# First expert's count and closing moved behind the mask multiplications, its tokens turned behind those of step 32

## The chip, the cores and the metric

One core of one Trainium2 chip runs the kernel. The metric is the device time of one execution in microseconds (us), as the median of several runs; less is better. The engines are named as in the profile: PE (TensorE matmul), PEld (its weight load), DVE (VectorE), ACT (ScalarE), POOL (GpSimd), SP (SyncE). DVE, ACT and POOL take their instructions in the order of the program.

## What is computed

Retention attention (8 batches, 8 heads, 576 positions, head size 64: scores with a decaying causal mask), whose output is read as 4608 tokens of 512 numbers, and then a mixture of 16 experts in 4 groups of 4. Each token goes to one expert: the best group, then the best expert in it.

```python
scores = scale * np.matmul(q, k.transpose(0, 1, 3, 2))
ret = scores * Dmat[None, :, :, :]          # gamma ** (i - j) for i >= j, else 0
x = np.matmul(ret, v)                       # turned to 4608 x 512
...
g_idx = np.argmax(x @ w_group, axis=1)
e_idx = np.argmax(xg @ w_expert[g], axis=1)
...
h = np.maximum(xg[mask_e] @ w1[g, e], 0.0)
ye = h @ w2[g, e]
out[tok_idx] = combined[:, None] * ye       # product of the two softmax weights
```

All in float32. An expert's layers are 512 by 1024 and 1024 by 512.

## The kernel before

The tokens are cut into 36 tiles of 128. A first loop over t (line 859) makes the attention, software-pipelined over the steps: in step t the scores of tile t + 1 are made by PE in the one PSUM tile `pss` (`scores`), and DVE multiplies them with the causal mask into `sT` (`masked`, two instructions). PE makes the products of tile t - 1 in the one PSUM tile pair `px` (`av` and `inter`), and DVE scales and copies them into `xT` (`turned`). `state` carries the sum over keys and values in `pst`, which ACT copies. Three tiles make a group: some steps behind its last tile, `logits` and `gate_pe` (PE), `choose` and `weigh` (DVE, with an exponential on ACT), and `places_pe` and `places` give each token of the group its expert and its row. POOL then stores the tokens, ordered by expert, in `xs` in HBM (`xnat_store`, an indirect DMA).

The experts' work begins before the last tiles are done. With PICK = 23, step 28 (r = 5) picks the expert with the most tokens so far (`pick(0)`), and its first 256 tokens (EARLY) are worked on as pass 0. Step 29 (r = 6) counts them and fixes them: `taken` is six small DVE instructions and one indirect DMA on POOL, which writes zeros over the rows behind the expert's last token (`xpad(0)`); `close` is three DVE instructions, which raise that expert's count so that later tokens stay apart from the early ones. Step 30 (r = 7) loads the expert's tokens from `xs` into `xb` (`xload(0)`, four DMAs on SP's queue and a small one for the tokens' numbers), and from there on each step loads a piece of weights (`load_piece`, two DMAs on SP's queue). Step 31 makes a mask of ids (`without`). Steps 34 and 35 (r = 11 and 12) turn `xb` into `xTf` by two block transposes on DVE (`xturn(0, 0, 2)` and `xturn(0, 1, 2)`). Step 34 also picks the second expert (`pick(1)`). The last step of the attention but one makes the first piece of the first layer (`layer1(0, 0)`, PE, line 598), which reads `xTf`.

Each engine but PE keeps the order in which the code is written (`pin`, line 94, which is also the line L117 that the profile shows for all of DVE, ACT, POOL and SP); PE's is fixed as well (`manual_schedule`). Waits between engines follow from the tiles that an instruction reads and writes. Behind the first loop come 16 passes over the experts and a last one for the rest of the first expert's tokens, in which nearly all time goes into matmuls.

Of the kernel before, what the change touches and what calls it, by code (L numbers as in the profile page):

```python
# [65 lines left out]
def moe_retention(ctx, tc, qk, kv, wgt, w1, w2, c_f, out):  # L66
# [117 lines left out]
    def ring(name):  # L184

        return gp.tile([P, NB * WQ], F32, name=name, tag="ring", bufs=4)

    def nblocks(p):
        return -(-CS[p] // 32)
# [4 lines left out]
    def xpair(nm):  # L194
        return [
            gp.tile([P, NKC, CMAX], F32R, name=f"xT{x_}_{nm}", tag="xT" + x_, bufs=2) for x_ in "hl"
        ]
# [63 lines left out]
    def xpad(p):  # L261

        row = apart("xs", pool.indirect_dma_start(
            out=xs, out_offset=bass.IndirectOffsetOnAxis(ap={0: pad0, 1: pad1}.get(p, pads[:, p % E : p % E + 1]), axis=0),
            in_=zero, in_offset=None, bounds_check=E * NS - 1, oob_is_err=False,
        ))
        if p == 1:
            placed.append(row)

    def pad(rows, e, n, cap):  # L270

        pd = sm.tile([P, 2], F32, name=f"pd_{rows.name}", tag="pd")
        dve.tensor_scalar(pd[:, 0:1], sln[:, 0:1], n, None, ALU.add)
        dve.tensor_scalar(pd[:, 1:2], pd[:, 0:1], float(cap), float(E * NS), ALU.is_ge, ALU.mult)
        dve.tensor_tensor(pd[:, 0:1], pd[:, 0:1], pd[:, 1:2], ALU.add)
        dve.scalar_tensor_tensor(rows, e, float(NS), pd[:, 0:1], ALU.mult, ALU.add)
# [4 lines left out]
    def xturn(p, part, of):  # L281

        if part == 0:
            xTs[p] = xpair(f"m{p}")
            if p == 0:

                xTf[p] = wp.tile([P, NKC, EARLY], F32, name="xTf_0", tag="wl1", bufs=3)
            else:
                xTf[p] = ring(f"xTf_{p}")[:, 0 : NKC * CMAX].rearrange("p (k c) -> p k c", k=NKC)
        nb = nblocks(p)  # L290
        b0, b1 = nb * part // of, nb * (part + 1) // of
        dve.transpose(
            xTf[p][:, :, 32 * b0 : 32 * b1].rearrange("p k (b t) -> p b k t", t=32),
            xg[p][:, b0:b1, 0:DQ].rearrange("p b (k f) -> p b k f", f=32),
        )
# [179 lines left out]
    def counted():  # L475

        return obs[-1][:, 0, :]
# [76 lines left out]
    def taken():  # L554

        f0, pc = picked[0]
        k2 = sm.tile([P, E], F32, name="k2")
        dve.tensor_tensor(k2, eah[0], pc, ALU.mult)
        c0 = sm.tile([P, 1], F32, name="c0")
        dve.tensor_reduce(c0, k2, AX.X, ALU.add)  # L560
        pad(pad0, f0, c0, EARLY)
        xpad(0)
        picked["c0"] = c0

    def close():

        c0 = picked["c0"]
        c2 = sm.tile([P, 1], F32, name="c2")
        dve.tensor_tensor(c2, room, c0, ALU.subtract)
        dve.tensor_scalar(c2, c2, 0.0, 2.0, ALU.max, ALU.min)  # L570
        dve.scalar_tensor_tensor(counted(), eah[0], c2, counted(), ALU.mult, ALU.add)
# [65 lines left out]
    with ExitStack() as ac:  # L637
# [41 lines left out]
        def more_masks():  # L679

            dve.tensor_copy(masks[:, 1], masks[:, 0])
            for par in range(2):
                dve.memset(masks[par * D : par * D + D, 1, par, D:P], 0.0)
# [11 lines left out]
        def make_gq(c):  # L695
            w = P if c < 4 else D
            for j in range(0, P, w):
                dve.tensor_tensor(
                    gqs[c][:, :, j : j + w], gqs[0][:, :, 0:w],
                    gc[:, c].unsqueeze(2).to_broadcast([P, 4, w]), ALU.mult,  # L700
                )
# [23 lines left out]
        def late_consts(t):  # L725
            if 0 < t < 5:
                make_gq(t)
            if t == 5:
                more_masks()
            if t == 3:  # L730
                dve.tensor_copy(ensb, cf[:, KC_ENS : KC_ENS + E])
                more_counts()
                dve.memset(counted(), 0.0)
                dve.memset(zero, 0.0)
# [39 lines left out]
        def masked(t):  # L774
            T = tiles[t]
            T["sT"] = ap.tile([P, 2, NP, P], F32, name=f"sT_{t}", tag="sT")
            mask = masks[:, T["m"]].unsqueeze(1).to_broadcast([P, 2, 2, P])
            for o in range(2):
                dve.tensor_tensor(
                    T["sT"][:, o].rearrange("p (i a) j -> p i a j", a=2),  # L780
                    pss[:, o].rearrange("p (i a j) -> p i a j", i=2, a=2), mask, ALU.mult,
                )
# [76 lines left out]
        for t in range(NT + 1):  # L859
            if t + LOADS - 1 < NT:  # L860
                loads(t + LOADS - 1, "a")
            now = t < NT
            r = t - PICK

            if last_of_group(t - 4):
                choose(t - 4)
            if last_of_group(t - 5):
                places(t - 5)
            if r == 8:
                without()  # L870
            if r in (11, 12):
                xturn(0, r - 11, 2)
            if t + 1 < NT:
                scale(t + 1)
            if t:
                av(t - 1)
            if t + LOADS - 1 < NT:
                loads(t + LOADS - 1, "b")
            if now:
                state(t)  # L880
            if t:
                inter(t - 1)
                turned(t - 1)
            if r == 6:
                taken()
                close()
            if last_of_group(t - 4):
                weigh(t - 4)
            if t + 1 < NT:
                scores(t + 1)  # L890
                masked(t + 1)
            late_consts(t)
            if now and 6 <= t:
                xnat_pe(t - 6)
                xnat_out(t - 6)
            if now and last_of_group(t - 2):
                logits(t - 2)
            if last_of_group(t - 3):
                gate_pe(t - 3)
            if now and last_of_group(t - 4):  # L900
                places_pe(t - 4)

            u = t - 6
            while 0 <= u and "sl" in tiles[tiles[u]["grp"][-1]] and not tiles[u].get("out"):
                tiles[u]["out"] = True
                u -= 1
            for u in range(max(u + 1, 0), t - 5):
                if now:
                    xnat_store(u)
            if r == 5:  # L910
                pick(0)
                expert_of(0)


            if r == 7:
                xload(0)
            if r == 11:
                pick(1)
                expert_of(1)
            if r > 6:  # L920
                load_piece(r - 7)
            if t == NT - 1:

                layer1(0, 0)
            if t == NT:
                ids(0)
# [576 lines left out]
```

## Time and profile before

| | us |
|---|---|
| median of 3 runs | 587.57 |
| lowest, highest | 586.05, 915.11 |
| profiled execution | 589.62 |
| its span, first to last instruction | 587.8 |
| PE busy in it | 571.2 (97%) |
| DVE busy in it | 425.8 (72%) |
| steps 28 to 35 in it | about 117 to 148 |

The timeline gives, for one engine, its instructions in order of time; like instructions that follow each other are one row with a count, and the length is from the first's start to the last's end. An instruction may start a little before the one ahead of it on its engine has ended. A wait that the profile puts down as "issue" is one for nothing that the profile shows. SPq is the queue that issues transfers; the length of such a row is that of issuing, not of the transfer.

### The profile page before, as it was taken

How to read it: one execution, taken by the hardware profiler on the slowest of the kernel's cores; microseconds unless marked ns; L12 is line 12 of the kernel's file. 1: busy time of each engine (PE TensorE's matmuls, PEld its weight loads, DVE VectorE, ACT ScalarE, POOL GpSimd, SP SyncE). 2: the span in 40 equal slices, each digit the busy share in tenths (PEclk: the TensorE clock that was granted, in tenths of full speed). 3: DMA queues.
4: the chain of work that ended last, by engine and by line, in shares of the span. 5: the costliest groups of instructions: out<-in, count | busy, mean ns of one | idle time of the engine just before them, and what ended most of it. 6: DMA issues, size and time to landing. Idle time of an engine off the chain costs nothing.

```text
span 587.8 us, 16858 instructions
## 1 busy us (share of the span) xinstructions
PE 571.2 (97%) x6057; PEld 535.8 (91%) x6057; DVE 425.8 (72%) x1003; ACT 326.3 (56%) x853; POOL 259.7 (44%) x391
## 2 busy tenths in 40 slices
PE   7999999999999999999999999999999999999994
PEld 5878788877779999999999999999999999999992
DVE  4877677788688768876768586776868768676782
ACT  5677777776456544454545454554545545455462
POOL 0022333233413046555564837355474654835643
PEclk7999999999999999999999999999999999999998
DMA  8999998979874944746656483937557494683921
GB/s 327 405 378 328 323 366 328 331 243 372 309 234 147 282 186 115 277 121 266 188 200 202 192 285 125 326 103 285 164 223 259 147 327 141 254 302 89 385 92 36
DMA packets 62410, 141.98 MB, mean 242 GB/s; under 512 B 9425, under 2 KB 30297, under 8 KB 62304
## 3 DMA queue, kind: packets, MB, share of 16 engines
q1 hardware_dynamic: 52944, 120.19, 59.0%
q0 software_dynamic: 9216, 20.28, 9.5%
q8 instruction: 73, 1.20, 0.8%
q14 instruction: 33, 0.27, 0.1%
q10 hardware_dynamic: 144, 0.05, 0.0%
HBM read 120.22 MB, written 24.81 MB: 247 GB/s over the span
## 4 chain that ended last, share of the span: by engine, by line
PE 87%; DVE 5%; issue 3%; DMA 2%; ACT 1%; POOL 1%; SPq 0%; POOLq 0%; DVEq 0%; another core or an unknown queue 0%
PE ph L612 31%; PE py L1016 10%; PE py L1018 10%; PE py L1017 10%; PE px L812 6%; PE pss L768 4%; PE pxt L378 3%; PE px L830 3%; PE pst L797 2%; PE pss L756 2%; PE plt L422 1%; DVE wl L117 1%; DVE sT L117 1%; POOL out L117 1%; PE ph L598 1%
## 5 line engine op out<-in xcount | busy, mean ns | idle before, releaser
L117 POOL DMA_INDIRECT out<-y,ii x151 | 164.0, 1086 | 66.4 <-issue 31.5
L117 DVE TENSOR_TENSOR wl<-r,wh 128x512 fp32r<-128x512 f32 x264 | 169.9, 685 | 5.8 <-ACT xt_last L117 2.6
L117 ACT ACTIVATE hh<-ph 128x256 fp32r<-128x256 f32 (+15 forms) x128 | 53.7, 420 | 200.4 <-PE ph L612 128.9
L117 ACT CAST wh<-r 128x512 fp32r<-128x512 f32 x264 | 149.1, 617 | 0.0
L612 PE MATMUL ph<-xTl_m,wh 128*128 128x324 f32 (+16 forms) x496 | 146.8, 296 | 0.3 <-DVE xTl_m L117 0.2
L612 PE MATMUL ph<-xTh_m,wh 128*128 128x324 f32 (+16 forms) x496 | 147.1, 297 | 0.0
L612 PE MATMUL ph<-xTh_m,wl 128*128 128x324 f32 (+16 forms) x496 | 146.6, 296 | 0.0
L1016 PE MATMUL py<-hh,wh 128*128 128x320 f32 (+19 forms) x480 | 143.0, 298 | 0.6 <-ACT hh L117 0.4
L1018 PE MATMUL py<-hl,wh 128*128 128x332 f32 (+14 forms) x480 | 142.2, 296 | 0.4 <-DVE hl L117 0.4
L1017 PE MATMUL py<-hh,wl 128*128 128x332 f32 (+14 forms) x480 | 141.8, 295 | 0.0
L117 DVE SCALAR_TENSOR_TENSOR hl<-ph,hh 128x256 fp32r<-128x256 f32 (+14 forms) x124 | 57.8, 467 | 99.9 <-ACT hh L117 54.9
L612 PEld LDWEIGHTS ph<-xTl_m,wh 128*128 128x128 f32 x496 | 93.6, 189 | 1.2 <-DVE xTl_m L117 0.7
L612 PEld LDWEIGHTS ph<-xTh_m,wh 128*128 128x128 f32 x496 | 93.6, 189 | 0.4 <-issue 0.2
L612 PEld LDWEIGHTS ph<-xTh_m,wl 128*128 128x128 f32 x496 | 93.7, 189 | 0.0
L117 POOL COPY pace<-hh 1x1 f32<-1x1 f32 x140 | 34.4, 246 | 131.8 <-ACT hh L117 120.9
L1016 PEld LDWEIGHTS py<-hh,wh 128*128 128x128 f32 x480 | 90.6, 189 | 1.3 <-ACT hh L117 1.2
L1018 PEld LDWEIGHTS py<-hl,wh 128*128 128x128 f32 x480 | 90.4, 188 | 0.9 <-DVE hl L117 0.9
L1017 PEld LDWEIGHTS py<-hh,wl 128*128 128x128 f32 x480 | 90.7, 189 | 0.0
L117 POOL DMA_INDIRECT xs<-xt,sl x33 | 32.7, 991 | 104.7 <-DVE xT L117 43.3
L117 ACT ACTIVATE vs<-b,cf 128x64 f32<-128x64 f32 x288 | 72.4, 336 | 8.0 <-DMA b<-in_kv 6.7
L117 DVE TENSOR_TENSOR sT<-pss,masks 128x512 f32<-128x512 f32 x72 | 46.0, 680 | 12.8 <-PE pss L756 7.0
L812 PE MATMUL px<-sT,vs 128*64 128x128 f32 x576 | 40.3, 283 | 0.1
(194 smaller groups left out, 614.3 us busy)
## 6 DMA issues: line engine op xcount, KB each, us to landing
r<-in_w SPq DMA_DIRECT2D x138, 512.0 KB
a<-in_qk SPq DMA_DIRECT2D x35, 512.0 KB
b<-in_kv SPq DMA_DIRECT2D x31, 512.0 KB
xb<-xs SPq DMA_DIRECT2D x20, 165.0 KB
xb<-xs SPq DMA_DIRECT2D x20, 148.5 KB
out<-y,ii POOLq DMA_INDIRECT x151
xb<-xs SPq DMA_DIRECT2D x12, 181.5 KB
b<-in_kv SPq DMA_DIRECT2D x6, 256.0 KB
```

The source lines that it names most:

```text
L117: i_ = f(*a, **k)
L378: pe.transpose(T["pxt"][:, i, :], T["xT"][:, i, :], ident)
L422: pe.matmul(plt[32 * i : 32 * i + 32], wgp[:, i, :], tiles[t]["xTg"][:, i], start=True, stop=True)
L612: pe.matmul(ph[:, :w], a[:, kc, cs], b[:, kc, :w], start=n == 0, stop=n == 3 * NKC - 1)
L756: pe.matmul(pss[:, o, i * P : i * P + P], T["kT"][r, i, :], T["qT"][r, i, :], start=True, stop=True,)
L768: pe.matmul(pss[k_, o, (i + par) * P + late * D : (i + par) * P + to], T["kT"][r, i + par, k_], T["qT"][r, i + par, late * D : to], start= ...
L797: pe.matmul(pst[o * D : o * D + D, i, :], T["k"][:, h, :], T["vs"][:, h, :], start=first and i == 0, stop=True, skip_group_check=True,)
L812: pe.matmul(px[g * D : g * D + D, o, s * P : s * P + P], T["vs"][:, 4 * s + 2 * g + o, :], T["sT"][:, o, 2 * s + g, :], start=s == 0, stop ...
L830: pe.matmul(px[g * D : g * D + D, o, s * P + r * w : s * P + r * w + w], st[rows, 2 * s + g, :], T["qT"][rows, 2 * s + g, r * w : r * w + ...
L1016: pe.matmul(py[:, :w0], wh[:, f % 2, ds_], hh[:, :w0], start=st_, stop=False)
L1017: pe.matmul(py[:, :w], wl[:, f % 2, ds_], hh[:, :w], start=False, stop=False)
L1018: pe.matmul(py[:, :w], wh[:, f % 2, ds_], hl[:, :w], start=False, stop=sp_)
```

## The change

In step 29, `taken` and `close` are written behind `scores` and `masked` of that step, which were ahead of `weigh` and `scores`. In step 32 (r = 9), behind its `scores` and `masked`, both transposes of the first expert's tokens follow each other; in steps 34 and 35 they are gone. Nothing is added or left out.

```diff
--- before.py
+++ after.py
@@ -868,8 +868,6 @@
                 places(t - 5)
             if r == 8:
                 without()
-            if r in (11, 12):
-                xturn(0, r - 11, 2)
             if t + 1 < NT:
                 scale(t + 1)
             if t:
@@ -881,14 +879,17 @@
             if t:
                 inter(t - 1)
                 turned(t - 1)
-            if r == 6:
-                taken()
-                close()
             if last_of_group(t - 4):
                 weigh(t - 4)
             if t + 1 < NT:
                 scores(t + 1)
                 masked(t + 1)
+            if r == 6:
+                taken()
+                close()
+            if r == 9:
+                xturn(0, 0, 2)
+                xturn(0, 1, 2)
             late_consts(t)
             if now and 6 <= t:
                 xnat_pe(t - 6)
```

PE, ACT, POOL and SP keep their order. On DVE two places change. The first is step 29, before the change. xT_27 from px_28 is the turn of tile 28, k2 to ob_8 are `taken` and `close`, sT_30 the two masks of tile 30, lg_26 the first instruction of `choose` for the group of tiles 24 to 26:

```order
L117 TENSOR_TENSOR xT_27_2417<-px_28_2492,gq1_115 128x4x128
L117 TENSOR_TENSOR k2_2522<-e0h_68,pc0_2459 128x16
L117 TENSOR_REDUCE c0_2524<-k2_2522 128x1
L117 TENSOR_SCALAR pd_pad0_79_2526<-cf_64,c0_2524 128x1
L117 TENSOR_SCALAR pd_pad0_79_2526<-pd_pad0_79_2526 128x1
L117 TENSOR_TENSOR pd_pad0_79_2526<-pd_pad0_79_2526 128x1
L117 SCALAR_TENSOR_TENSOR pad0_79<-f00_2468,pd_pad0_79_2526 128x1
L117 TENSOR_TENSOR c2_2534<-cf_64,c0_2524 128x1
L117 TENSOR_SCALAR c2_2534<-c2_2534 128x1
L117 SCALAR_TENSOR_TENSOR ob_8_2385<-e0h_68,c2_2534,ob_8_2385 128x16
L117 TENSOR_TENSOR sT_30_2554<-pss_109,masks_113 128x512 x2
L117 TENSOR_REDUCE lg_26_2572<-pl_26_2565 128x60
```

And with the change:

```order
L117 TENSOR_TENSOR xT_27_2417<-px_28_2492,gq1_115 128x4x128
L117 TENSOR_TENSOR sT_30_2538<-pss_109,masks_113 128x512 x2
L117 TENSOR_TENSOR k2_2541<-e0h_68,pc0_2459 128x16
L117 TENSOR_REDUCE c0_2543<-k2_2541 128x1
L117 TENSOR_SCALAR pd_pad0_79_2545<-cf_64,c0_2543 128x1
L117 TENSOR_SCALAR pd_pad0_79_2545<-pd_pad0_79_2545 128x1
L117 TENSOR_TENSOR pd_pad0_79_2545<-pd_pad0_79_2545 128x1
L117 SCALAR_TENSOR_TENSOR pad0_79<-f00_2468,pd_pad0_79_2545 128x1
L117 TENSOR_TENSOR c2_2553<-cf_64,c0_2543 128x1
L117 TENSOR_SCALAR c2_2553<-c2_2553 128x1
L117 SCALAR_TENSOR_TENSOR ob_8_2385<-e0h_68,c2_2553,ob_8_2385 128x16
L117 TENSOR_REDUCE lg_26_2572<-pl_26_2565 128x60
```

The masks of tile 30 moved ahead of the nine instructions; what stands behind both is the same. The second place is the end of step 32 and the start of step 33, before the change. lg_29 to ob_9 are `choose` for the group of tiles 27 to 29, xT_30 from px_32 is the turn of tile 32:

```order
L117 TENSOR_TENSOR sT_33_2811<-pss_109,masks_113 128x512 x2
L117 TENSOR_REDUCE lg_29_2834<-pl_29_2823 128x60
L117 TENSOR_REDUCE mx_29_2836<-lg_29_2834 128x15
L117 TENSOR_TENSOR df_29_2838<-lg_29_2834,mx_29_2836 128x60
L117 SCALAR_TENSOR_TENSOR oh_29_2842<-df_29_2838,cf_64 128x60
L117 TENSOR_REDUCE m2_29_2844<-oh_29_2842 128x15
L117 TENSOR_TENSOR oh_29_2842<-oh_29_2842,m2_29_2844 128x60
L117 TENSOR_TENSOR ob_9_2680<-oh_29_2842 128x48
L117 TENSOR_TENSOR xT_30_2720<-px_32_2857,gq1_115 128x4x128
```

With the change:

```order
L117 TENSOR_TENSOR sT_33_2811<-pss_109,masks_113 128x512 x2
L117 STREAM_TRANSPOSE xTf_0_2816<-xb_0_2665 128x4x4x32 x2
L117 TENSOR_REDUCE lg_29_2839<-pl_29_2828 128x60
L117 TENSOR_REDUCE mx_29_2841<-lg_29_2839 128x15
L117 TENSOR_TENSOR df_29_2843<-lg_29_2839,mx_29_2841 128x60
L117 SCALAR_TENSOR_TENSOR oh_29_2847<-df_29_2843,cf_64 128x60
L117 TENSOR_REDUCE m2_29_2849<-oh_29_2847 128x15
L117 TENSOR_TENSOR oh_29_2847<-oh_29_2847,m2_29_2849 128x60
L117 TENSOR_TENSOR ob_9_2680<-oh_29_2847 128x48
```

The two transposes (xTf_0) came in between the masks of tile 33 and `choose`. In steps 34 and 35 they stood, before the change, like this (k01 to e1i are `pick(1)`):

```order
L117 TENSOR_REDUCE ob_10_2935<-ob_9_2680 128x16
L117 STREAM_TRANSPOSE xTf_0_2939<-xb_0_2665 128x4x4x32
L117 TENSOR_TENSOR xT_33_2977<-px_33_2950,gq2_116 128x4x128
L117 TENSOR_TENSOR sT_35_2995<-pss_109,masks_113 128x512 x2
L117 SCALAR_TENSOR_TENSOR k01_3021<-pc1_3019,cf_64 128x16
L117 SCALAR_TENSOR_TENSOR k01_3021<-e0h_68,k01_3021 128x16
L117 TENSOR_REDUCE m01_3024<-k01_3021 128x1
L117 TENSOR_SCALAR e1h_69<-k01_3021,m01_3024 128x16
L117 TENSOR_TENSOR k11_3027<-e1h_69,cf_64 128x16
L117 TENSOR_REDUCE f01_3029<-k11_3027 128x1
L117 CAST e1i_71<-f01_3029 128x1
L117 STREAM_TRANSPOSE xTf_0_2939<-xb_0_2665 128x4x4x32
```

With the change both are gone there, and the rest follows in the same order:

```order
L117 TENSOR_REDUCE ob_10_2940<-ob_9_2680 128x16
L117 TENSOR_TENSOR xT_33_2978<-px_33_2951,gq2_116 128x4x128
L117 TENSOR_TENSOR sT_35_2996<-pss_109,masks_113 128x512 x2
L117 SCALAR_TENSOR_TENSOR k01_3022<-pc1_3020,cf_64 128x16
L117 SCALAR_TENSOR_TENSOR k01_3022<-e0h_68,k01_3022 128x16
L117 TENSOR_REDUCE m01_3025<-k01_3022 128x1
L117 TENSOR_SCALAR e1h_69<-k01_3022,m01_3025 128x16
L117 TENSOR_TENSOR k11_3028<-e1h_69,cf_64 128x16
L117 TENSOR_REDUCE f01_3030<-k11_3028 128x1
L117 CAST e1i_71<-f01_3030 128x1
L117 TENSOR_TENSOR xT_33_2978<-px_34_3047,gq3_117 128x4x128
```

## Rows read from the trace of the kernel before

**Rows 1.** The page of the profile: the span, PE's and PEld's busy time, PE's busy share in 40 equal slices in tenths, the queue that brings instructions (packets, MB, share of 16 engines), and the engines' shares of the chain that ended last.

```profile
span 587.8 us, 16858 instructions
...
PE 571.2 (97%) x6057; PEld 535.8 (91%) x6057; DVE 425.8 (72%) x1003; ACT 326.3 (56%) x853; POOL 259.7 (44%) x391
...
PE   7999999999999999999999999999999999999994
...
q8 instruction: 73, 1.20, 0.8%
...
PE 87%; DVE 5%; issue 3%; DMA 2%; ACT 1%; POOL 1%; SPq 0%; POOLq 0%; DVEq 0%; another core or an unknown queue 0%
```

**Rows 2.** Timeline of DVE from 121 to 130 us, steps 29 to 31. Columns: start and length in us, engine, line and operation, out<-in with its shape, count, and in brackets the engine's idle time before it and what ended that. The row at 121.64 is the first instruction of `taken`, the one at 123.13 the last of `close`.

```profile
121.03 0.69 DVE L117 TENSOR_TENSOR xT<-px,gq 128x512 f32<-128x512 f32 x1 [1.07 <-PE px L830]
121.64 0.16 DVE L117 TENSOR_TENSOR k<-e0h,pc 128x16 f32<-128x16 f32 x1
...
123.13 0.23 DVE L117 SCALAR_TENSOR_TENSOR ob<-e0h,c,ob 128x16 bf16<-128x16 f32 x1
123.28 1.28 DVE L117 TENSOR_TENSOR sT<-pss,masks 128x512 f32<-128x512 f32 x2
124.48 0.40 DVE L117 TENSOR_REDUCE lg<-pl 128x60 f32<-128x240 f32 x1
...
127.84 1.26 DVE L117 TENSOR_TENSOR sT<-pss,masks 128x512 f32<-128x512 f32 x2
```

**Rows 3.** Timeline of PE from 120 to 130 us, columns as above; L768 are the scores, L830 the products with the state.

```profile
120.56 1.02 PE L768 MATMUL pss<-a 64*64 64x128 f32 x32
...
123.91 0.67 PE L830 MATMUL px<-a,st 64*64 64x128 f32 x16
124.61 0.91 PE L768 MATMUL pss<-a 64*64 64x128 f32 x13
125.94 0.68 PE L768 MATMUL pss<-a 64*64 64x64 f32 x19 [0.42 <-issue]
...
128.75 0.67 PE L830 MATMUL px<-a,st 64*64 64x128 f32 x16
129.24 0.85 PE L768 MATMUL pss<-a 64*64 64x128 f32 x32
```

**Rows 4.** Waits between 123.5 and 126 us: who waited for whom, us in total, times, the longest.

```profile
PEld pss L768 <- DVE sT L117: 0.3, 1, 0.3
```

**Rows 5.** Timeline of POOL: the pad of the first expert and the store behind it.

```profile
123.11 0.97 POOL L117 DMA_INDIRECT xs<-zero,pad  x1 [2.69 <-DVE c L117]
...
124.55 0.99 POOL L117 DMA_INDIRECT xs<-xt,sl  x1 [0.28 <-POOL xt L117]
```

**Rows 6.** Timeline of SP's queue from 123 to 176 us: start and length of the issuing, and the count. xb at 127.62 is the first expert's tokens, xb at 166.26 the next expert's; r are weights.

```profile
127.62 2.14 SPq L117 DMA_DIRECT2D xb<-xs  x4
...
130.81 20.06 SPq L117 DMA_DIRECT2D r<-in_w  x14
166.26 1.89 SPq L117 DMA_DIRECT2D xb<-xs  x4
```

**Rows 7.** Waits of SP's queue between 123 and 140 us, columns as in rows 4.

```profile
SPq L117 <- DMA xs<-xt,sl: 4.1, 1, 4.1
SPq L117 <- PE px L830: 3.3, 1, 3.3
```

**Rows 8.** Timeline of DVE from 134 to 173 us, columns as in rows 2. The first two rows of xTf are the transposes that the change moves, the last is the next expert's.

```profile
134.27 1.29 DVE L117 TENSOR_TENSOR sT<-pss,masks 128x512 f32<-128x512 f32 x2 [1.05 <-PE pss L768]
135.47 0.40 DVE L117 TENSOR_REDUCE lg<-pl 128x60 f32<-128x240 f32 x1
...
137.22 0.21 DVE L117 TENSOR_TENSOR ob<-oh 128x48 bf16<-128x48 f32 x1
137.92 0.69 DVE L117 TENSOR_TENSOR xT<-px,gq 128x512 f32<-128x512 f32 x1 [0.49 <-PE px L830]
...
139.46 1.26 DVE L117 TENSOR_TENSOR sT<-pss,masks 128x512 f32<-128x512 f32 x2
...
141.40 0.71 DVE L117 STREAM_TRANSPOSE xTf<-xb 128x512 f32<-128x512 f32 x1 [0.16 <-issue]
...
145.17 0.70 DVE L117 STREAM_TRANSPOSE xTf<-xb 128x512 f32<-128x512 f32 x1
...
172.58 1.30 DVE L117 STREAM_TRANSPOSE xTf<-xb 128x512 f32<-128x512 f32 x2 [1.01 <-DMA xb<-xs]
```

**Rows 9.** Timeline of PE from 139 to 148 us; L812 are the products of the masked scores with the values, L797 the state, L435 turns the gate's logits, L598 is `layer1(0, 0)`.

```profile
139.02 1.09 PE L812 MATMUL px<-sT,vs 128*64 128x128 f32 x16
139.94 0.63 PE L797 MATMUL pst<-vs,b 128*64 128x64 f32 x16
...
140.99 0.64 PE L768 MATMUL pss<-a 64*64 64x64 f32 x32
...
145.17 0.49 PE L435 MATMUL pl<-cf,lt 128*128 128x128 f32 x3
145.93 1.99 PE L598 MATMUL ph<-xTf,r 128*128 128x256 f32 x8 [0.27 <-DVE xTf L117]
```

**Rows 10.** Timeline of ACT from 136 to 139 us: the exponential inside `choose`, and the copy of the state.

```profile
136.41 0.25 ACT L117 ACTIVATE ex<-df 128x60 f32<-128x60 f32 x1 [0.77 <-DVE df L117]
...
138.48 0.34 ACT L117 COPY st<-pst 128x256 f32<-128x256 f32 x1
```

## The prediction

> **What bounds the kernel now.** I read the page first. PE is busy for 97% of a span of 587.8 us, and 87% of the chain that ended last is PE; DVE has 5% of it [rows 1]. So a change on DVE is worth what PE stops waiting for, and nothing else. I therefore looked at the places where PE waits for DVE in the steps that are edited, about 120 to 147 us into the span. There are two.
>
> The first is in step 29. DVE turns px of tile 28 at 121.03, then does the nine small instructions of `taken` and `close` (from 121.64 to 123.36), and only then masks the scores of tile 30 (123.28 to 124.56) [rows 2]. PE has a single `pss`: it wrote those scores from 120.56 to 121.58 and can't write tile 31's before DVE has read them. Tile 31's scores begin at 124.61, 0.05 us after the mask ends [rows 3], and the weight load ahead of them waited 0.3 us for sT [rows 4]. The reader is to see that the nine instructions are long, and that the wait they make on PE is short: PE had other work until 124.4.
>
> The second is before `layer1(0, 0)`: its first matmul at 145.93 waited 0.27 us for the second transpose of the first expert's tokens, which DVE did from 145.17 to 145.87 [rows 8, 9].
>
> **Part 1: the count and closing go behind the mask.** DVE does the same nine instructions and two mask multiplications in another order, so it reaches the first instruction of `choose` at 124.48 either way. The mask of tile 30 starts when its scores are there, behind the turn, at 121.64, which is 1.64 us earlier. What PE gets of that: elsewhere its scores start 0.49 us after the product with the state ahead of them (128.75 to 129.24); in step 29 it was 0.70 us (123.91 to 124.61) [rows 3]. So PE wins 0.21 us. It doesn't keep it: one step later DVE, which has not moved, masks tile 31 from 127.84 to 129.10 [rows 2], and with the same 0.05 us of handing over PE can't start tile 32's scores before 129.15. Before they started at 129.24. What is left is **-0.09 us**. Ends of this term: 0 and the 0.3 us of the wait [rows 4]; the nine instructions whole, 1.64 us, would be the most that could be had if PE had nothing else to do.
>
> PE's own gaps in that place bear on it too: in tile 31's scores there is a gap of 0.42 us with "issue" as its cause, between 125.52 and 125.94 [rows 3], in which it waits for nothing that the profile shows. If that gap stays where it is in time, even the 0.21 us is lost there, and the term is 0. [...]
>
> **What part 1 makes late.** `taken` issues a DMA, the pad of the first expert. Nine instructions start later by the mask, 1.20 us (123.28 to 124.48). POOL issues the pad at 123.11 and the store of tile 23's tokens behind it at 124.55 [rows 5]; both move by 1.20. On SP the load of the first expert's tokens (`xload(0)`) waited 4.1 us for such a store's landing [rows 7] and went out at 127.62 [rows 6]; it moves to 128.82, and with it the weight loads queued behind it, from 130.81. Two of the first expert's eight weight loads wait for PE anyway (3.3 us [rows 7]), so the queue is level again there. The first weights are wanted at 145.93, 15 us after the first load's issue. So this costs 0; if the cover were gone it would cost PE up to 1.20 us.
>
> **Part 2: both transposes go ahead of `choose` of step 33.** They leave the places at 141.40 (0.71 us) and 145.17 (0.70 us) and stand behind the mask of tile 33 [rows 8]. Side by side two take 1.30 us (the row at 172.58), and a DVE instruction starts about 0.08 us before the one ahead of it ends (124.48 against 124.56), so what follows moves by 1.22 us. In a row:
> - `choose` starts at 136.69 instead of 135.47, and its last instruction ends at 138.65 instead of 137.43.
> - The turn of tile 32 was idle 0.49 us for PE before its start at 137.92. That idle time takes part of the shift: it starts at 138.57, 0.65 us late, and ends at 139.26.
> - PE has one px. Its products of tile 33 at 139.02 [rows 9] must wait for that turn: about 139.31, 0.29 us late.
> - The mask of tile 34 starts at 139.46 + 0.65 = 140.11 and ends at 141.37. PE's scores of tile 35, at 140.99 before [rows 9], start at 141.42: **+0.43 us** (this holds the 0.29).
> - ACT's exponential of that `choose` moves from 136.41 to 137.63, and the copy of the state behind the eight scalings from 138.48 to 139.70, ending at 140.05 [rows 10]. PE's next state product stood at 139.94 and now stands at 140.23, so it isn't held, with 0.18 us to spare.
> - From there DVE is ahead: it has no transpose in its next two steps. `layer1(0, 0)` finds its tokens done since about 136.8, so its wait goes: **-0.27 us**.
>
> Without the overlap of 0.08 us (shift 1.30, the turn 0.81 late) the scores come at 141.58, +0.59; with all of it hidden behind other work of PE it is 0. I take 0.43 since it goes by starts, as the rows show them.
>
> Whether the tokens are there in time: no row shows when they landed, since the transposes were too late to wait. The next expert's load bounds it from above: issued from 166.26 to 168.15, its tokens, 12 blocks of 32 against 8, let the transpose begin at 172.58 [rows 6, 8]. That is 6.32 us from the first issue, 4.43 from the end of the last. With 128.82, and 127.62 + 2.14 + 1.20 = 130.96, the first expert's land by 135.14 to 135.39; the transposes come up at about 135.39. So no wait, by a margin near zero on that bound and of several us if landing is quick. [...]
>
> **The sum**: -0.09 + 0.43 - 0.27 = +0.07 us. The profiled execution took 589.62 us around its span of 587.8; with the change 589.7. The median of the runs is 587.57, 2.05 us less; the same sum there gives 587.6. From the second of the 40 slices to the last but one PE is busy for nine tenths or more [rows 1], so what is won or lost there reaches the end nearly whole.
>
> **Rivals.**
> - *Faster*: the shift of `choose` is hidden. Then the wait before `layer1(0, 0)` goes for nothing (-0.27) and the wait of step 29 whole (-0.3): 587.0. For it: both waits are on record [rows 4, 9]. Against it: there is one `pss` and one px, and the mask of tile 34 would have to end by about 140.94; it ended at 140.72 before, so only 0.2 us of a shift are free.
> - *Slower*: DVE takes its instructions in order, and if the tokens land after 135.4 the transposes hold `choose`, the turn of tile 32 and the masks. Its price is one us per us of lateness. If the landing is later by the whole 1.20 us that part 1 adds, the sum is +1.3: 588.8. For it: the bound of the next expert's load leaves no margin. Against it: that load is half as large again, and was issued beside other traffic.
> - *It doesn't do what it says*: the 0.42 us gap takes part 1's lead, and both masks of tiles 34 and 35 hold PE as before: the terms cancel within 0.2 us, 587.8. This can't be told from the forecast by the time, only in the trace.
>
> **How the numbers follow.** Forecast with the third rival: 0.64. Faster by half a us or more: 0.18. Slower by that: 0.14. Something that these rows don't show, of more than 2%: 0.04. Two per cent are 11.8 us, about what a measurement of this kernel can tell from no change, and over forty times the wait before `layer1(0, 0)`; so the chances are faster 0.02, within 2% 0.96, slower 0.02. The range goes from the nine instructions won whole, 587.57 - 1.64 = 585.9, to the transposes lost whole, 587.57 + 1.22 = 588.8; it also takes in the spread of the two low runs, 586.05 and 587.57. The forecast's own range is 587.0 to 588.0.
>
> **What would show it.** In the changed trace: tile 31's scores without a wait for sT, starting at about 124.4; tile 32's still at about 129.15; the pad about 1.2 us later, and the token load with it; two transposes side by side ahead of `choose` without a wait for DMA; the turn of tile 32 without a wait for PE, and PE waiting for DVE at tile 35's scores; no wait for xTf at `layer1(0, 0)`, which starts within 0.3 us of 145.93. Wrong would be: a DMA wait at the transposes, or `layer1(0, 0)` more than 0.5 us off.

## The result, and the profile after

Median after 591.44 us (588.48 to 595.64, 20 runs), before on the same chip 587.96: ratio 1.0054, 95% interval 1.0034 to 1.0073. The kernel became about half a per cent slower, 3.2 us by that ratio (the two medians lie 3.5 us apart), which is within 2% but outside the range of the prediction: 587.57 by that ratio is 590.7, where 588.8 was the upper end.

The page of the changed kernel, profiled in an execution of 590.35 us; its lines answer to [rows 1]:

```profile
span 588.6 us, 16856 instructions
...
PE 570.3 (97%) x6057; PEld 534.3 (91%) x6057; DVE 426.7 (72%) x1003; ACT 326.8 (56%) x853; POOL 257.9 (44%) x391
...
PE   7999999998999999999999999999999999999995
...
PE 85%; DMA 5%; DVE 3%; issue 3%; ACT 2%; POOL 1%; SPq 1%; POOLq 0%; DVEq 0%; ACTq 0%
```

PE does the same work, but one slice (the tenth, around 140 us) has fallen from 9 to 8, and DMA has 5% of the chain of work where it had 2%. The timeline of DVE shows both edits; the rows at 121.39 to 124.08 answer to [rows 2], the others to [rows 8]:

```profile
120.72 0.69 DVE L117 TENSOR_TENSOR xT<-px,gq 128x512 f32<-128x512 f32 x1 [1.06 <-PE px L830]
121.39 1.29 DVE L117 TENSOR_TENSOR sT<-pss,masks 128x512 f32<-128x512 f32 x2
122.60 0.16 DVE L117 TENSOR_TENSOR k<-e0h,pc 128x16 f32<-128x16 f32 x1
...
124.08 0.23 DVE L117 SCALAR_TENSOR_TENSOR ob<-e0h,c,ob 128x16 bf16<-128x16 f32 x1
...
133.83 1.29 DVE L117 TENSOR_TENSOR sT<-pss,masks 128x512 f32<-128x512 f32 x2 [0.89 <-PE pss L768]
137.27 1.30 DVE L117 STREAM_TRANSPOSE xTf<-xb 128x512 f32<-128x512 f32 x2 [2.15 <-issue]
138.50 0.37 DVE L117 TENSOR_REDUCE lg<-pl 128x60 f32<-128x240 f32 x1
...
140.17 0.21 DVE L117 TENSOR_TENSOR ob<-oh 128x48 bf16<-128x48 f32 x1
140.29 0.68 DVE L117 TENSOR_TENSOR xT<-px,gq 128x512 f32<-128x512 f32 x1
```

The mask now stands ahead of the nine small instructions, as it should. DVE stands idle for 2.15 us ahead of the transposes, and `choose` behind them begins at 138.50 where 136.69 was forecast. This profile names "issue" for the wait, that is, nothing that it shows; the chain of waits of the same execution, in order of time (start, length, what), names what came ahead of it:

```profile
125.50 4.75 DMA xs<-xt,sl
...
131.98 3.80 DMA xb<-xs
135.78 1.48 issue
137.27 1.30 DVE xTf L117 x2
```

So the transposes wait for the tokens `xb` (a second profile of this kernel names that load outright, below), and these for the store of one tile's tokens into `xs`, which took 4.75 us from its start on POOL. The expectations below call it the store of the token list. The timeline of POOL (pad, then store) answers to [rows 5]:

```profile
124.06 0.97 POOL L117 DMA_INDIRECT xs<-zero,pad  x1 [3.94 <-DVE c L117]
...
125.50 0.99 POOL L117 DMA_INDIRECT xs<-xt,sl  x1 [0.28 <-issue]
```

and that of SP's queue to [rows 6]:

```profile
130.37 1.98 SPq L117 DMA_DIRECT2D xb<-xs  x4
...
133.35 21.45 SPq L117 DMA_DIRECT2D r<-in_w  x14
170.40 1.89 SPq L117 DMA_DIRECT2D xb<-xs  x4
```

Of SP's waits, [rows 7] have become (from 123 to 140 us):

```profile
SPq L117 <- DMA xs<-xt,sl: 8.0, 1, 8.0
SPq L117 <- PE pss L768: 0.4, 1, 0.4
```

The weight loads behind the tokens, which had 3.3 us of waiting for PE to spare, wait 0.4 us for it now; no wait of `layer1(0, 0)` for weights follows. Pad and store are 0.95 us later than before. The load is 2.75 us later. Before, store to load was 127.62 - 124.55 = 3.07 us; now it is 4.87. What it does to PE (rows as in [rows 3, 9]):

```profile
123.65 0.67 PE L830 MATMUL px<-a,st 64*64 64x128 f32 x16
124.14 0.85 PE L768 MATMUL pss<-a 64*64 64x128 f32 x32
...
126.19 0.18 PE L509 MATMUL pp<-ob,up 128*128 128x48 bf16 x1 [0.41 <-DVE ob L117]
...
128.90 0.90 PE L768 MATMUL pss<-a 64*64 64x128 f32 x32
...
140.43 0.18 PE L509 MATMUL pp<-ob,up 128*128 128x48 bf16 x1 [1.90 <-DVE ob L117]
...
141.03 1.97 PE L812 MATMUL px<-sT,vs 128*64 128x128 f32 x16 [0.32 <-DVE xT L117]
142.79 1.06 PE L797 MATMUL pst<-vs,b 128*64 128x64 f32 x16
143.78 0.95 PE L830 MATMUL px<-a,st 64*64 64x128 f32 x16
...
149.71 1.89 PE L598 MATMUL ph<-xTf,r 128*128 128x256 f32 x8
```

PE waits 1.90 us for the `ob` that `choose` makes. Then its products with the masked scores (L812) take 1.97 us where they took 1.09 [rows 9], and `layer1(0, 0)` starts at 149.71, 3.78 us after its place in [rows 9]. The lengthening goes with the clock. The table of stretches (length, each engine's busy time and instructions, granted clock, DMA share, GB/s), of the changed kernel:

```profile
136.00:142.00 6.00, 3.67 (x75) 3.06 (x71) 4.39 (x16) 2.42 (x10) 1.32 (x3) 0.92 1.01 360
142.00:148.00 6.00, 5.68 (x101) 4.53 (x99) 3.90 (x11) 4.00 (x12) 0.99 (x1) 0.80 1.00 396
```

and of the kernel before:

```profile
136.00:142.00 6.00, 5.78 (x161) 5.32 (x156) 5.01 (x18) 4.40 (x17) 1.44 (x4) 1.00 1.02 411
```

PE was busy for only 3.67 of the first 6 us, and the granted clock then was 0.50 for about 3.4 us: read in smaller stretches it is 0.51 from 141.0 to 141.5, 0.50 to 144.4 and 0.98 to 145.0. Three groups pay for it: L812, L797 and L830 are 0.88, 0.43 and 0.28 us longer than the same groups elsewhere (1.09 and 0.63 in [rows 9], 0.67 at 123.65), together 1.59 us. With L812 itself starting 2.01 us late, that is nearly all of the 3.78.

The two profiled spans differ by only 0.8 us, since each execution is one of many: that of before took 589.62, 1.66 above its median, that of after 590.35, 1.09 below. What before lost, it lost late: lined up at one PE instruction near 130 us, the changed kernel is 5.0 us behind before from 180 to 510 us, and 1.2 us behind at 582. Of the difference 1.65 us stand at 579.78, in the second layer's last pass:

```profile
579.78 0.50 PE L1005 MATMUL py<-wh,hhn 128*128 128x512 f32 x1 [1.65 <-ACT hhn L117]
```

### The profile page after: what moved, and what is told of

The parts are those of the page before. It is cut to its first block, busy times and chain, and to the rows that moved or that the text cites. A ratio compares the mean times of both kernels' runs of the same rounds, so it can differ in the third digit from the quotient of the medians.

```text
span 588.6 us, 16856 instructions
## 1 busy us (share of the span) xinstructions
PE 570.3 (97%) x6057; PEld 534.3 (91%) x6057; DVE 426.7 (72%) x1003; ACT 326.8 (56%) x853; POOL 257.9 (44%) x391
## 4 chain that ended last, share of the span: by engine, by line
PE 85%; DMA 5%; DVE 3%; issue 3%; ACT 2%; POOL 1%; SPq 1%; POOLq 0%; DVEq 0%; ACTq 0%
PE ph L612 32%; PE py L1017 11%; PE py L1018 11%; PE py L1019 11%; PE px L812 5%; PE pss L768 3%; PE pxt L378 3%; DMA b<-in_kv 3%; PE px L830 2%; PE pst L797 2%; DMA xb<-xs 2%; PE plt L422 1%; PE ph L598 1%; ACT wh L117 1%; POOL out L117 1%
## 5 line engine op out<-in xcount | busy, mean ns | idle before, releaser
L117 POOL COPY pace<-hh 1x1 f32<-1x1 f32 x140 | 32.7, 234 | 133.8 <-ACT hh L117 122.7
L812 PE MATMUL px<-sT,vs 128*64 128x128 f32 x576 | 40.3, 283 | 0.8 <-issue 0.4
```

What stands on the lines that cost most here:

```text
L117: i_ = f(*a, **k)
L812: pe.matmul(px[g * D : g * D + D, o, s * P : s * P + P], T["vs"][:, 4 * s + 2 * g + o, :], T["sT"][:, o, 2 * s + g, :], start=s == 0, stop ...
```

## The experiments

Theory A: only both parts together cost time, since part 1 makes the tokens late and part 2 wants them early. Rivals: B, part 1 alone costs it; C, part 2 alone does, because two transposes in a row occupy DVE. For what makes the tokens late by more than the 1.2 us of part 1 there were then A1, a packet of the queue that the profile calls instruction (the fetch) meets the store, against A2, the change costs its half per cent however that fetch falls.

**Both parts taken singly, and together with a later turn.** First the kernel with part 1 alone:

```diff
+            if r in (11, 12):
+                xturn(0, r - 11, 2)
...
-            if r == 9:
-                xturn(0, 0, 2)
-                xturn(0, 1, 2)
```

> Part 1 alone: the count and closing behind the mask, the transposes where they were before. Theory A (the tokens land too late for transposes that stand in step 32, and only both parts together make DVE wait): no DMA wait at the transposes, PE as before, ratio to before 0.998 to 1.002. Theory B (part 1 is at fault: the pad, the token load and the weights behind it come late): most of the loss of the change, +3 us, ratio about 1.005. Theory C (the DVE time of two transposes ahead of choose is at fault): ratio 1.000.

Measured: ratio 1.0004 (0.9979 to 1.0029). The load goes out at 130.93, 4.82 us behind its store, as late as in the changed kernel, and no transpose waits for it (DVE):

```profile
140.71 0.71 DVE L117 STREAM_TRANSPOSE xTf<-xb 128x512 f32<-128x512 f32 x1 [0.15 <-issue]
```

Late tokens alone cost nothing. B falls. Then part 2 alone:

```diff
+            if r == 6:
+                taken()
+                close()
             if last_of_group(t - 4):
...
-            if r == 6:
-                taken()
-                close()
```

> Part 2 alone: both transposes in step 32, the count and closing ahead of the mask as before. Theory A: the tokens land at about 132, as in the trace of before, and the transposes come up at about 135.5; no DMA wait, PE loses 0.4 us at the scores of tile 35 and wins 0.3 at the first expert's first layer, ratio 0.999 to 1.002. Theory B: 1.000. Theory C: the loss of the change, +3 us, ratio about 1.005, with no DMA wait ahead of the transposes.

Measured: 1.0007 (0.9979 to 1.0035). The load at 128.52 is 3.29 us behind its store; DVE turns without a wait, and PE waits for DVE much as the prediction's part 2 has it:

```profile
135.68 1.29 DVE L117 STREAM_TRANSPOSE xTf<-xb 128x512 f32<-128x512 f32 x2
136.90 0.37 DVE L117 TENSOR_REDUCE lg<-pl 128x60 f32<-128x240 f32 x1
```

```profile
138.83 0.18 PE L509 MATMUL pp<-ob,up 128*128 128x48 bf16 x1 [0.18 <-DVE ob L117]
...
139.43 0.77 PE L812 MATMUL px<-sT,vs 128*64 128x128 f32 x10 [0.32 <-DVE xT L117]
```

C falls as a cause of half a per cent. Both parts, but the transposes one step later:

```diff
-            if r == 9:
+            if r == 10:
```

> Both parts, but the transposes one step later, behind the mask of tile 34. Theory A: they come up at about 140.7, behind the tokens' landing at 133 to 137; no wait for DMA, no fall of the granted clock between 135 and 150, and no stall before the first layer: ratio 0.998 to 1.001. Theory B: still +3 us, ratio about 1.005. Theory C: the 1.3 us of DVE now hold the next products, about +0.4 us or more.

Measured: 1.0008 (0.9984 to 1.0031), transposes at 142.40 without a wait, though the load went out at 133.68, 5.1 us behind its store. The changed kernel again, on the chip of these three:

> The changed kernel once more. Theory A: DVE again waits ahead of the transposes, by 1 to 3 us from one execution to the next as the store before the token load lands early or late; ratio about 1.005. If the wait of the first profile was an accident of that one execution, it is absent here, and the cause of the median's +3 us lies elsewhere.

Measured: 1.0119 (1.0078 to 1.0160). Here the profile names the load, and PE waits and slows down as in the first profile (DVE, then PE):

```profile
136.75 1.30 DVE L117 STREAM_TRANSPOSE xTf<-xb 128x512 f32<-128x512 f32 x2 [2.20 <-DMA xb<-xs]
```

```profile
139.90 0.20 PE L509 MATMUL pp<-ob,up 128*128 128x48 bf16 x1 [2.47 <-DVE ob L117]
...
140.51 1.98 PE L812 MATMUL px<-sT,vs 128*64 128x128 f32 x16 [0.27 <-DVE xT L117]
```

Three kernels in which the tokens come early or the turn comes late are level with before, and the whole change is not: theory A.

**What in part 1 matters.** `taken`, which issues the pad, goes back ahead of the mask; `close` stays behind it, and the transposes in step 32:

```diff
+            if r == 6:
+                taken()
             if last_of_group(t - 4):
...
             if r == 6:
-                taken()
                 close()
```

> Both transposes in step 32 and the closing behind the mask, but the count with its pad stays ahead of the mask, so that the pad goes to POOL early. Theory A (the pad is late, so the tokens are, and the early transposes wait for them): the token load is issued within 3.5 us of the store as in the trace of before, no DMA wait at the transposes, ratio 0.998 to 1.002. If the closing's three instructions or the order of the mask are at fault: ratio about 1.005 to 1.012.

Measured: 1.0014 (0.9995 to 1.0034). Load at 127.57, transposes at 134.30 without a wait. So of part 1 it is `taken` that counts, the one that issues the pad, behind which the store stands.

**The clock.** The changed kernel, with eight matmuls more on constants where PE would idle:

```diff
+            if r == 10:
+                pf = ps_sm.tile([P, 4, P], F32, name="pf", tag="sm")
+                for i in range(8):
+                    pe.matmul(pf, ones, ones.unsqueeze(1).to_broadcast([P, 4, P]), start=True, stop=True)
```

> The changed kernel with eight matmuls of constants (128x512, bf16, into a tile that nobody reads) on PE where it stands idle for the turn of the group behind the transposes, in step 33; they add work that is not in the reference. Theory A with a fall of the clock as part of the price: the granted clock stays at its upper level between 135 and 150, and 1.5 to 3 us of the loss go, ratio about 1.003 to 1.006 where the changed kernel had 1.012 on the last chip and 1.005 on the first. If the clock's fall costs nothing by itself: the same ratio as the changed kernel, or 1 us worse.

Measured: 1.0075 (1.0047 to 1.0103). In its profile L812 behind the transposes takes 1.09 us (at 140.26) and not 1.97, but the transposes waited only 0.47 us in that execution, and the eight matmuls themselves take 1.89 us of PE. It shows neither how much of the loss the clock is, nor that filling helps. The clock's part stays an account of single profiles.

**DVE's occupancy by itself.** The kernel before, with two transposes of a tile that has long been there, in the new place:

```diff
+            if r == 9:
+                xd = wp.tile([P, NKC, EARLY], F32, name="xd", tag="wl1", bufs=3)
+                for i in range(2):
+                    dve.transpose(
+                        xd[:, :, P * i : P * i + P].rearrange("p k (b t) -> p b k t", t=32),
+                        gqs[0].rearrange("p b (k f) -> p b k f", f=32),
+                    )
```

> The kernel of before with two more transposes of the same size in step 32, of a table that has long been there into a tile that nobody reads: the DVE time ahead of choose without the tokens; they add work that is not in the reference. Theory A: this costs what the prediction gave it, 0.4 to 0.6 us, ratio 1.000 to 1.002. Theory C (occupancy): +3 us and more, ratio 1.005 to 1.012.

Measured: 1.0019 (1.0000 to 1.0038), with the same 0.18 and 0.32 us of PE's waits as in part 2 alone. That is 0 to 2.2 us, and agrees with the 0.43 us of the prediction.

**Why the store lands late.** In the DMA records one packet of the instruction queue stands out, one of the 73 in [rows 1], 1.20 MB in all, so 16.4 KB each on average. The store's packets are in q0 together with the pad's, 160 in all: by their sizes 80 are the pad's and 80 the store's, 64 of these with 4224 bytes each, 0.27 MB. Of the kernel before, from 124.5 to 127.3 us all of them are there and no other queue but q1 (queue: packets, MB, share of 16 engines):

```profile
q1 hardware_dynamic: 150, 0.29, 33.4%
q0 software_dynamic: 160, 0.33, 31.3%
```

and from 127.4 to 127.7 us only this, behind the store:

```profile
q8 instruction: 1, 0.02, 18.6%
```

In the changed kernel the store's packets run into that packet, from 127.4 to 129.1 us:

```profile
q0 software_dynamic: 47, 0.14, 21.2%
q8 instruction: 1, 0.02, 5.4%
```

and from 128.3 to 130.4 us the last three packets of the store begin, with no other transfer beside them but the rest of that one packet. The first of the three starts at 129.01, and that packet ends at 129.02:

```profile
q0 software_dynamic: 3, 0.01, 2.2%
```

The fetch keeps its time (its packet starts at 127.46 before, at 127.56 now); the store moved into it. To move it away, the 8 warm matmuls at the start of the program, whose results nobody reads, are cut into 72 narrower ones of about the same work, 128 PE instructions more with their weight loads, in the changed kernel:

```diff
-        for i in range(WARM):
-            pe.matmul(pw, ones, ones.unsqueeze(1).to_broadcast([P, 4, P]), start=True, stop=True)
+        for i in range(WARM + 64):
+            pe.matmul(pw[:, 0, 0:56], ones, ones[:, 0:56], start=True, stop=True)
```

> The changed kernel with the eight warming matmuls at the start cut into 72 narrower ones of about the same columns in sum, so that PE's instruction lines are fetched half a line earlier or later all through the program. Theory A1 (the store ahead of the token load lands late because a line of 16 KB for PE is fetched at that moment, 127.5 us): the load is issued 3.1 to 3.5 us after the store instead of 4.6 to 4.9, the wait at the transposes shrinks from 2.2 us to under 1.2, and most of the loss goes: ratio 1.000 to 1.005. Theory A2 (the store lands late for another reason, the traffic of that time): still 4.6 us and more, and the ratio of the changed kernel, 1.005 to 1.012.

Measured: 0.9975 (0.9952 to 0.9998); 2.88 us from store to load, and no wait:

```profile
128.45 1.29 DVE L117 STREAM_TRANSPOSE xTf<-xb 128x512 f32<-128x512 f32 x2
```

The same edit in the kernel before:

> The kernel before with its 8 warm matmuls cut into 72 of 128x56: 128 more PE instructions at the program's start, so that PE's instruction blocks of 16 KB are fetched elsewhere against the work; it is the control of e7_shift. Theory A1 (the change costs time only where such a fetch falls on the store of the token list): the ratio is that of e7_shift within its error, 0.995 to 1.000, so that the change costs nothing in this phase. Theory A2 (the change costs its half per cent in any phase, and the other warm form alone wins time): about 0.993 against the kernel before, half a per cent under e7_shift.

Measured: 0.9997 (0.9972 to 1.0021). Then 256 PE instructions more instead of 128, in the changed kernel and in the one before:

```diff
-        for i in range(WARM):
-            pe.matmul(pw, ones, ones.unsqueeze(1).to_broadcast([P, 4, P]), start=True, stop=True)
+        for i in range(WARM + 128):
+            pe.matmul(pw[:, 0, 0:30], ones, ones[:, 0:30], start=True, stop=True)
```

> The changed kernel with the 8 warm matmuls cut into 136 of 128x30: 256 more PE instructions, one whole instruction block, so that the blocks' borders lie at the same work as in the changed kernel. Theory A1: the fetch is back on the store, from the store's issue to the token load's it is 4.5 us or more, xTf waits for the load and the clock falls; 0.5 to 1.2% slower than e10_line_before. Theory A2, with the gain coming from small warm matmuls: like e7_shift, 2.9 us from store to load and no loss against e10_line_before.

> The kernel before with the same 136 warm matmuls of 128x30: the control of e9_line. Both theories: within 0.5% of the kernel before, the start perhaps 1 us later since the small matmuls take longer in sum; the token load about 3 us behind its store.

Measured: 1.0067 (1.0027 to 1.0108) for the changed kernel, 1.0012 (0.9986 to 1.0038) for its control: 0.55% between them, with both errors 0.07 to 1.03%. With the small matmuls too, the wait is back with 256 instructions more (DVE of the changed one; 4.62 us from store to load, 1.09 us of PE's wait for `ob`, then L812 in 1.88 us):

```profile
139.80 1.30 DVE L117 STREAM_TRANSPOSE xTf<-xb 128x512 f32<-128x512 f32 x2 [1.32 <-DMA xb<-xs]
```

The changed kernel once more beside them:

> The changed kernel once more, so that e7_shift to e10_line_before have it on the same chip. Every theory: 1.004 to 1.013 against the kernel before; by A1 with more than 4 us from the list's store to the token load, by the rival to it (the list's later start alone) with about 3 us.

Measured: 1.0052 (1.0023 to 1.0081), runs from 587.17 to 593.76. The profiled one took 587.30, among its fastest; there the store took 4.11 us, the load's last packet ended at 136.82, and the transposes came up at 137.59 without a wait:

```profile
136.36 1.29 DVE L117 TENSOR_TENSOR sT<-pss,masks 128x512 f32<-128x512 f32 x2 [0.98 <-PE pss L768]
137.59 1.30 DVE L117 STREAM_TRANSPOSE xTf<-xb 128x512 f32<-128x512 f32 x2
```

So the wait is not in every execution: the margin is near zero, and the spread falls to both sides of it. Last, the shift in both kernels on one chip, and 64 PE instructions more (`WARM + 32` matmuls of 128x102) in the changed kernel:

> The kernel of e7_shift (the changed kernel with 128 more PE instructions at the start), on one chip with its control. Theory A1 (the meeting of fetch and store is the whole cost): equal to shift_both_b within 0.25%, token load about 3 us behind its store, no wait at the transposes. Theory A2 (the change costs something in any phase): 0.3 to 0.8% slower than shift_both_b.

> The kernel of e8_shift_before (the kernel before with the same 128 more PE instructions), the control. Both theories: 0.997 to 1.002 against the kernel before; A2 needs it 0.3% or more under shift_both_a.

> The changed kernel with its 8 warm matmuls cut into 40 of 128x102: 64 more PE instructions, so that the fetch comes a quarter of a block earlier, some 0.5 to 1 us behind the store's issue and not 1.5 to 2. A1: 3.4 to 4.0 us from store to token load, no wait or one under 0.5 us at the transposes, ratio between e7_shift's and the changed kernel's, 0.998 to 1.004. A2: as the changed kernel, 1.005 or more.

Measured: 0.9971 (0.9949 to 0.9993) with the change, 0.9949 (0.9933 to 0.9965) without; medians 578.83 and 578.30 us. The ratios lie 0.22% apart (with both errors -0.05 to 0.49%), the medians 0.09%. That is as A1 has it, but the error reaches into the 0.3 to 0.8% of A2; e7_shift and e8_shift_before, on two chips, lie 0.22% apart the other way. With 64 more: 1.0001 (0.9983 to 1.0019), 2.88 us from store to load, transposes without a wait. Its store was better off than A1 forecast (3.4 to 4.0 us), since the fetch came still earlier in that execution, 0.08 us ahead of the store. Three more sizes were missed: e7_shift and shift_both_b came out faster than expected, e5_fill slower, and the load of e10_line_before went out 3.78 us behind its store, where about 3 were expected.

All profiles in one table, by the start of the fetch's packet against the store's issue (both from one profile each):

| kernel | fetch behind the store, us | store to load, us | wait of the transposes, us |
|---|---|---|---|
| e7_shift, shift_both_a, quarter | -0.44, -0.37, -0.08 | 2.88, 2.88, 2.88 | none |
| e8_shift_before, shift_both_b | 0.93, 1.13 | 3.72, 3.87 | none (turned in steps 34, 35) |
| again2, again | 1.53, 1.57 | 4.11, 4.63 | none, 2.20 |
| e1_part1, e3_step33 | 1.58, 1.58 | 4.82, 5.12 | none (turned later) |
| e5_fill | 1.66 | 4.27 | 0.47 |
| e9_line, after | 2.05, 2.06 | 4.62, 4.87 | 1.32, 2.15 |
| e4_taken_stays, e10_line_before | 2.51, 2.82 | 3.39, 3.78 | none |
| e6_dummy, before, e2_part2 | 2.85, 2.91, 2.95 | 3.61, 3.07, 3.29 | none |

Against the 2.88 us of the first row, where the fetch starts ahead of the store, one that starts 0.9 to 1.1 us behind the store's issue goes with 0.8 to 1.0 us more, and one that starts 1.5 to 2.1 us behind with 1.2 to 2.2 us more. In the seven profiles of that second kind the last three to five packets of the store start within 0.02 us of the end of the fetch's packet, behind a pause of 0.2 to 1.1 us. That the fetch held them is the author's reading of these times; by what means is not shown. In the last two rows, where the fetch starts 2.5 us or more behind, the store's last packet ended before the fetch's did, so the 0.2 to 0.9 us more there aren't a hold of this kind; what they are stays open. Only PE's number of instructions was changed for it, so the fetch goes with PE's instructions: with 256 more it starts 2.05 us behind the store, as without them (2.06), and with 128 or 64 more 0.08 to 0.44 us ahead of it. What the expectations call a line or a block of 256 instructions is, by these runs, the step that brings the fetch back to its place.

The same profiles show what the wait costs. Lined up with the profile of before as above, I read how late PE is at the instruction that before had at 200 us: 5.0 us in the first profile of the changed kernel, 4.8 in again, 2.8 in e9_line and 0.0 in again2, for waits of 2.15, 2.20, 1.32 us and none. In the other twelve it lies between 1.2 us early and 0.8 us late. Of the granted clock, the means from 136 to 142 and from 142 to 148 us are 0.92 and 0.80 in the first profile of the changed kernel, 0.79 and 0.64 in again, 1.00 and 0.72 in e9_line, and 1.00 in before, again2 and quarter. The L812 behind the wait takes 1.97, 1.98 and 1.88 us in the three with these waits; in the other profiles the sixteen take 1.09 us from 130 to 150 us, but for one row of fifteen with 1.25 in e6_dummy.

## Why the prediction was wrong

- **The path and part 1.** Right. The turn ahead of the mask came 0.31 us early in this execution (120.72 against 121.03 [rows 2]). Tile 31's scores start at 124.14 without a wait for sT, 0.49 us behind the product ahead of them as forecast. PE then gives the lead back, 0.41 us of it to `ob`, and tile 32's scores start at 128.90, which with the 0.31 added is level with 129.24 [rows 3]. The gap of 0.42 us in tile 31's scores is gone (the 32 scores at 124.14 are one row); in the profile of before no instruction packet lies in it, the nearest end at 122.95 and start at 127.46. Part 1 alone: 1.0004.
- **What part 1 makes late: the step that failed.** The prediction moved pad, store, load and weights all by the same 1.20 us and put the cost at nothing. For pad and store that is right: 0.95 us later, 1.26 against the rest of this execution. The time from store to landing was taken as a constant, and it isn't one: the store took 3.07 us to the load's issue before, 4.87 after, since about 1 us later its last packets meet the fetch (from 127.56), which before began at 127.46, when the store's packets were all in (by 127.3). So the load moved by 2.75 us and not by 1.20. [rows 1] has that packet's queue; the prediction did not ask which transfers its packets meet.
- **Whether the tokens are there in time: the same error, carried on.** Its upper bound was 135.14 to 135.39; in the changed kernel the load's last packet ended at 136.5, and DVE was ready for the transposes at about 135.1 (133.83 + 1.29). The two signs of being wrong that the prediction named, a wait for DMA at the transposes and `layer1(0, 0)` more than 0.5 us off, both came. The shortest stores here took 2.88 us to the load's issue, those that met the fetch 4.1 to 5.1. The load went out at 130.37, 1.55 us behind the 128.82 of the prediction, and the margin of several us that it left to a quick landing was not there.
- **The load's own length**, which the bound also held fixed. From issue to last packet the load itself took 4.2 us before and 6.1 after, so of the 4.7 us by which its last packet came later, 1.8 are the store's length and 2.0 the load's own. Over all seventeen profiles the load took 3.7 to 4.3 us in the five where no instruction packet starts during it, and 4.7 to 6.1 in the twelve where one does; weights lie beside it too, and which of the two holds it was not separated. Without the store's part there was no wait even so: in e7_shift, shift_both_a and quarter the load took 4.7 to 5.1 us with such a packet in it.
- **Part 2.** Right in kind, and its 0.43 us for DVE's occupancy lies within what the runs allow: 1.0007 for part 2 alone and 1.0019 for the dummy transposes, 0 to 2.2 us. PE's 0.18 us of waiting for `ob` wasn't in its list. The wait ahead of `layer1(0, 0)` went as forecast: its row at 149.71 has none.
- **The rival that came true** is the slower one, and it was given 0.14 beside a margin called near zero. Its price, one us per us of lateness and 1.3 us in all, was too small as well: DVE waited 2.15 us and not 1.20, and PE's idle time was followed by about 3.4 us at a granted clock of 0.50, in which three groups took 1.59 us more in the profiled execution.
- **The faster and the null rival.** The whole 0.3 us of step 29 did not come, and the terms of part 1 and part 2 do cancel within the error once the meeting is taken away (shift_both_a against shift_both_b: 0.09% by the medians). So the sum of +0.07 us fits the change without the fetch, but only within about 0.5%, 3 us.

Left open: how the loss divides between wait and clock over many executions; why the changed kernel had 1.0119 on one chip and 1.005 on two others; and why the shift alone, without the change, made the kernel before faster by 0.5% on one chip (0.9949) and not on another (0.9997). In the first profile of the changed kernel PE also loses 1.1 us between 170 and 180 us, where the next expert's transposes wait 2.28 us for their tokens; e10_line_before, without the change, loses about as much there behind 2.15 us, so it isn't put down to the change. No version here beats both kernels by the change: the shifted changed kernel does (0.9975, 0.9971), but the shifted kernel before is no slower.

## What to carry to other kernels

A transfer that moves by a microsecond need not keep its length (here 3.07 us became 4.87): look in the DMA records for what it will now run beside, and for packets of the instruction queue above all, since here that packet kept its time within 0.1 us (127.46, 127.56) while the store moved by 0.95. Where a use is moved earlier and its store-and-load chain later in one change, a margin that comes out as near zero can be a loss in a good part of the executions, as here in two of three profiles of the changed kernel; take the parts apart, or leave the instruction that issues the transfer where it was (`taken` ahead of the mask: 1.0014). Price such a wait with the clock that PE may lose behind it, not only with its length: here 1.59 us at a clock of 0.50, behind a wait of 2.15.

## What the hardware showed unexpectedly

In the seven profiles in which one 16.4 KB packet of the instruction queue, 1.1 to 1.9 us long, started 1.5 to 2.1 us behind a store of 80 packets, the last three to five of these started at that packet's end, and from the store to the load it took 4.1 to 5.1 us instead of 2.88. Adding instructions at the program's start, 128 on PE at about the same work, moved this meeting and with it the time of the changed kernel by 0.8% between ratios (1.0052 or 1.0054 against 0.9975 or 0.9971); the kernel before moved by 0.0 to 0.5% with the same edit. So here the place of that packet weighed more than the edit itself, whose ratios away from that meeting lie 0.22% from its control's, once above and once below.
